# A planned kernel whose planner is told of the eight transfers in flight, and may give early small work to GpSimd

## The chip, the cores and the metric

The kernel runs on one core of a Trainium2 chip. The metric is device time in microseconds (us) of one execution, as a median over runs. The engines are named as in the profile: PE is TensorE, DVE is VectorE, ACT is ScalarE, POOL is GpSimd, SP is SyncE, which here only issues transfers (DMAs). All matrix products are in float32, and most of them are made of three products of high and low parts.

## The reference

```python
scores = (q @ k^T) / 8                          # 4 batches x 8 heads, 576 x 576, head size 64
keep   = scores >= max(scores) - tau            # per row
attn   = softmax of the kept scores             # exp(s - max) / (sum + 1e-9)
x = concat over heads of (attn @ v)             # 2304 tokens x 512
h = x @ w_in;   x = (h * clip(h + 3, 0, 6) / 6) @ w_out          # 512 -> 2048 -> 512
h = x @ w_in2;  x = (h * sigmoid(1.702 * h)) @ w_out2            # 512 -> 2048 -> 512
```

## The kernel before

**Stages.** Attention is worked in 16 units of two heads (function `unit`). The first four (`u < FULL`) are the early ones: their scores are plain float32 products of `g` (or `kqv`) with the keys `kqv` (L653, L669), and their probabilities are turned by TensorE (L743) and multiplied with the values (L785). The other twelve split q and k into high and low parts (L637) and partly turn the probabilities through DRAM (L754, L757, L759; their products are L802). Beside attention the first half of the first feed-forward layer is computed (`moe_a`, L862 and L887), then its second half (`moe_b`), then the second layer (`moe2`, L1024 and L887). The weights come as 64-bit words and are decoded to floats by `decode`: a load `wrawstg` (L470), two ACT copies (L480, and L427 in place), three DVE steps (a clamp L481, a shift L483, a merge L484) and a POOL addition.

**One score tile.** The function `soft` follows a score product into one of two PSUM tiles `ps`: the row maximum (R, DVE, L685), the threshold `th` = maximum - tau (TH, L686, 128x1), the exponential (X, ACT, L688) and the masking with its sum (M, DVE, L689), which needs `th` and frees the `ps` tile. So PE can be at most two score tiles ahead of M.

**What sets the order.** Nothing is scheduled by hand. `Plan` holds every operation with an engine, a planned cost and what it reads and writes. `order` runs the plan as a list schedule, `latest` turns it round into priorities, and `settle` repeats both under a list of numbers (KICKS and SHAKES): a positive number disturbs the priorities as a random seed, a negative one, -n, moves operation n to the engine that its `alt` names. The result is one fixed order for each engine, and engines wait for each other by semaphores only. The dictionary `PORT` names the operations of DVE and POOL that the plan keeps from overlapping.

**Fillers.** After planning, `fill` puts small products of the constant `two` (L1187) wherever the planned order leaves PE without work, about one for every 0.216 us of the planned gap less 0.3 us. They compute nothing that is used. Before has 35 of them, 70 records in the trace, since a float32 product of this kind has two.

**Transfers.** `move` adds an issue on SP (or ACT) and the transfer itself. The built program gives every transfer one of eight semaphores in turn, and an issue waits until the transfer that had the same semaphore, eight issues earlier, has landed. In `order` of before a transfer waits for its issue and its data alone. SP takes its list in order, so one late transfer can hold all that stand behind it.

## Time and profile before

| what | us |
|---|---|
| median of 3 runs | 1064.68 (1060.67 to 1068.29) |
| profiled execution, its own time | 1060.78 |
| span of the profiled execution | 1059.0 |
| PE busy | 1045.0 |
| fillers among that (L1187, 70 records) | 11.2 |
| DVE / ACT / POOL busy | 718.5 / 631.0 / 518.9 |

A busy PE is the union of its matmul records, and their ends are modelled; a wait of PE shows as a gap, or as an idle time with its releaser behind a row. In the 40 slices of the page PE stands at 8 in the first and at 9 in all that follow but the last, which ends after the last product. The granted TensorE clock is 9 (0.98 to 1.00) throughout.

### The profile page before, as it was taken

How to read it: one execution, taken by the hardware profiler on the slowest of the kernel's cores; microseconds unless marked ns; L12 is line 12 of the kernel's file. 1: busy time of each engine (PE TensorE's matmuls, PEld its weight loads, DVE VectorE, ACT ScalarE, POOL GpSimd, SP SyncE). 2: the span in 40 equal slices, each digit the busy share in tenths (PEclk: the TensorE clock that was granted, in tenths of full speed). 3: DMA queues.
4: the chain of work that ended last, by engine and by line, in shares of the span. 5: the costliest groups of instructions: out<-in, count | busy, mean ns of one | idle time of the engine just before them, and what ended most of it. 6: DMA issues, size and time to landing. Idle time of an engine off the chain costs nothing.

```text
span 1059.0 us, 20374 instructions
## 1 busy us (share of the span) xinstructions
PE 1045.0 (99%) x7470; PEld 955.4 (90%) x7470; DVE 718.5 (68%) x1542; ACT 631.0 (60%) x1272; POOL 518.9 (49%) x597
## 2 busy tenths in 40 slices
PE   8899999999999999999999999999999999999998
PEld 6677888899879988999999999989988989899888
DVE  7898888767777872677765333888787585563544
ACT  4889677666666664666554224766665675344433
POOL 4579888776867663755574225441422431001000
PEclk9999999999999999999999999999999999999999
DMA  7434465645564535445744211527553561320202
GB/s 229 117 101 149 136 182 164 191 139 156 160 183 127 157 110 173 131 144 178 218 145 139 60 59 59 165 80 228 166 169 119 178 193 35 119 86 35 95 1 76
DMA packets 87109, 141.79 MB, mean 134 GB/s; under 512 B 8544, under 2 KB 51168, under 8 KB 85472
## 3 DMA queue, kind: packets, MB, share of 16 engines
q1 hardware_dynamic: 86784, 140.41, 44.2%
q8 instruction: 59, 0.97, 0.4%
q14 instruction: 42, 0.34, 0.1%
q10 hardware_dynamic: 224, 0.07, 0.0%
HBM read 97.32 MB, written 43.12 MB: 133 GB/s over the span
## 4 chain that ended last, share of the span: by engine, by line
PE 88%; DVE 4%; DMA 3%; ACT 2%; issue 1%; SPq 1%; POOL 1%; ACTq 0%; DVEq 0%; POOLq 0%
PE py L887 26%; PE pm L862 19%; PE pm L1024 15%; PE pm L887 9%; PE ps L637 6%; PE pm L802 6%; PE pm L743 5%; PE pm L785 1%; PE ps L669 1%; DMA kqv<-in_k_dram 1%; DMA wrawstg<-in_w1i_dram 1%; DVE outlring L430 1%; DVE e L689 0%; DMA wrawstg<-in_w1o_dram 0%; SPq L589 0%
## 5 line engine op out<-in xcount | busy, mean ns | idle before, releaser
L887 PE MATMUL py<-g,outhring 128*128 128x512 f32 (+2 forms) x1152 | 286.4, 336 | 0.7 <-DVE g L430 0.7
L887 PEld LDWEIGHTS py<-g,outhring 128*128 128x128 f32 x1152 | 192.4, 188 | 16.6 <-DVE g L430 1.9
L887 PE MATMUL py<-g,outlring 128*128 128x512 f32 (+2 forms) x576 | 193.2, 335 | 0.0
L862 PE MATMUL pm<-xh,inhring 128*128 128x256 f32 (+1 forms) x512 | 153.4, 300 | 0.2
L862 PE MATMUL pm<-xl,inhring 128*128 128x256 f32 (+1 forms) x512 | 150.8, 295 | 0.0
L862 PE MATMUL pm<-xh,inlring 128*128 128x256 f32 (+1 forms) x512 | 150.7, 294 | 0.0
L1024 PE MATMUL pm<-outhring,inhring 128*128 128x256 f32 x512 | 144.7, 283 | 0.5 <-ACT p L427 0.4
L1024 PE MATMUL pm<-outlring,inhring 128*128 128x256 f32 x512 | 143.9, 281 | 0.1
L1024 PE MATMUL pm<-outhring,inlring 128*128 128x256 f32 x512 | 143.6, 280 | 0.0
L685 DVE TENSOR_REDUCE nm<-ps 128x1 f32<-128x576 f32 x144 | 107.0, 752 | 35.8 <-PE ps L637 30.1
L430 POOL TENSOR_TENSOR g<-t,g 128x256 fp32r<-128x256 f32 (+1 forms) x104 | 87.8, 850 | 81.7 <-ACT g L427 74.8
L887 PEld LDWEIGHTS py<-g,outlring 128*128 128x128 f32 x576 | 108.1, 188 | 10.1
L689 DVE SCALAR_TENSOR_TENSOR e<-ps,th,e 128x576 f32<-128x576 f32 x128 | 102.4, 810 | 21.5 <-ACT e L688 20.1
L874 DVE SCALAR_TENSOR_TENSOR t<-t,pm 128x256 f32<-128x256 f32 (+1 forms) x128 | 57.2, 450 | 86.7 <-ACT t L873 86.2
L430 POOL TENSOR_TENSOR g<-tc,g 128x512 fp32r<-128x512 f32 x24 | 32.5, 1355 | 161.9 <-ACT g L427 160.0
L688 ACT ACTIVATE e<-ps,nm 128x576 f32<-128x576 f32 x128 | 92.7, 739 | 31.9 <-DVE nm L685 27.8
L430 POOL TENSOR_TENSOR wmstg<-wmstg,wrstg 128x512 uint32<-128x512 uint32 x48 | 66.9, 1393 | 91.1 <-DVE wmstg L484 69.5
L873 ACT ACTIVATE t<-pm,half 128x256 f32<-128x256 f32 (+1 forms) x128 | 63.4, 500 | 80.3 <-PE pm L862 77.6
L887 PE MATMUL pm<-g,outhring 128*128 128x256 f32 (+1 forms) x512 | 107.3, 300 | 0.0
L1024 PEld LDWEIGHTS pm<-outhring,inhring 128*128 128x128 f32 x512 | 96.7, 189 | 5.1 <-ACT p L427 1.0
L1024 PEld LDWEIGHTS pm<-outlring,inhring 128*128 128x128 f32 x512 | 96.8, 189 | 3.2 <-DVE outlring L430 0.3
L862 PEld LDWEIGHTS pm<-xh,inhring 128*128 128x128 f32 x512 | 96.5, 188 | 2.1 <-PE pm L1187 0.7
(114 smaller groups left out, 2397.2 us busy)
## 6 DMA issues: line engine op xcount, KB each, us to landing
turned<-tr SPq DMA_DIRECT2D x12, 1024.0 KB, 3.9
et<-turned SPq DMA_DIRECT2D x48, 256.0 KB, 6.2
wrawstg<-in_w1i_dram SPq DMA_DIRECT2D x16, 512.0 KB, 4.0
wrawstg<-in_w1o_dram SPq DMA_DIRECT2D x16, 512.0 KB, 3.6
wrawstg<-in_w2i_dram SPq DMA_DIRECT2D x16, 512.0 KB, 3.8
wrawstg<-in_w2o_dram SPq DMA_DIRECT2D x16, 512.0 KB, 3.9
qk<-in_k_dram SPq DMA_DIRECT2D x24, 288.0 KB, 3.8
qk<-in_q_dram SPq DMA_DIRECT2D x24, 288.0 KB, 3.4
```

The source lines that it names most:

```text
L430: return lambda: (nc.vector if eng == DVE else nc.gpsimd).tensor_tensor(out=o(), in0=a(), in1=b(), op=op)
L637: nc.tensor.matmul(ps.t[:, i, :SH], qss[hd].t[:, q0:q0 + P], w[hd].t[:, i * SH:(i + 1) * SH], start=a, stop=z)
L685: add(DVE, 672, K("R", s), "R", lambda: nc.vector.tensor_reduce(out=nm.t[:, c], in_=ps.t[:, :, :SH], op=ALU.max, axis=AX.XY, negate=True), ...
L688: add(ACT, 624, K("X", s), "X", lambda: nc.scalar.activation(out=ev(), in_=ps.t[:, :, :SH], func=ACTF.Exp, bias=nm.t[:, c]), [ps, (nm, s)] ...
L689: add(DVE, 736, K("M", s), "M", lambda: nc.vector.scalar_tensor_tensor(out=ev(), in0=ps.t[:, :, :SH], scalar=th.t[:, c], in1=ev(), op0=ALU ...
L743: nc.tensor.transpose(pt.t[:kn, o:o + P], e_of[s].t[:, keys(k)], id_b.t)
L802: nc.tensor.matmul(pv[p].t[64 * hd:64 * hd + 64, :CH[p][1]], v_(k, hd), x, start=k == 0, stop=k == 4)
L862: nc.tensor.matmul(ph.t[:, :n], a, v, start=(cc == 0 and i == 0), stop=(cc == KC - 1 and i == 2))
L873: add(ACT, 93 + act(n), K("RL"), "RL", lambda: nc.scalar.activation(out=tt_(), in_=pt(), func=ACTF.Relu, scale=1.0 / 6.0, bias=half_b.t), ...
L874: add(DVE, dve(n), K("GT"), "GT", lambda: nc.vector.scalar_tensor_tensor(out=tt_(), in0=tt_(), scalar=1.0, in1=pt(), op0=ALU.min, op1=ALU. ...
L887: nc.tensor.matmul(py.t[:, :n], a, v, start=(st and i == 0), stop=(sp and i == 2))
L1024: nc.tensor.matmul(o.t[:, :n], u.t[:, ws], v.t[:, xv], start=(st and kk == 0 and i == 0), stop=(sp and kk == 1 and i == 2), skip_group_che ...
```

## The change

1. `order` gets a list of SP's transfers. An issue on SP waits in the plan for the transfer eight issues earlier (LANES = 8) and the latency of a transfer. Transfers of ACT's queue are not in that list.
2. At the start the first unit's keys go through ACT's queue; tau and the first half of q, which were there, go through SP's.
3. The planned size factor of a weight load is 1.7 where it was 1.4.
4. TH gets POOL as its other engine (it was ACT).
5. KICKS and SHAKES are other numbers, so every engine's order is another. Thirteen of their moves put work on POOL: 8 thresholds TH, 3 scalings of q (128x256, 128x512, 128x384) and 2 clamps (128x512). There are 49 fillers where there were 35. Otherwise the engines have the same instructions.

```diff
-CAPS, BANKS = (2, 2, 3, 4), 4
+CAPS, BANKS, LANES = (2, 2, 3, 4), 4, 8
...
 KICKS = (
-    838826498, 483723856, 648238324, 249340718, 651019405, 283728814,
+    185786211, 131810043, 105014005, 620353508, 1009081972, 162601711, 396413032, 546200070, 621028586, -184, 226485323, 975211561,
...
+        issued, late, fin = [], [], [None] * n
...
+            if e == SP and cost[o] and len(issued) >= LANES:
+                x = fin[issued[-LANES] + 1]
+                if x is None:
+                    late.append(o)
+                    continue
+                if x + LAT[DMA, SP] > t:
+                    est[o] = x + LAT[DMA, SP]
+                    heappush(p, (est[o], o))
+                    continue
...
+            if e == SP and cost[o]:
+                issued.append(o)
+            elif e == DMA:
+                fin[o] = end
+                for h in late:
+                    heappush(pend[SP], (est[h], h))
+                late = []
...
-    move(-30000, "tau", 4 * P, lambda: nc.scalar.dma_start(out=tau_b.t, in_=tau), [], [tau_b], ACT)
+    move(-30000, "tau", 4 * P, lambda: nc.sync.dma_start(out=tau_b.t, in_=tau), [], [tau_b])
...
-        move(time - 15000, "WL", 8 * P * DM * 1.4, load, [], [raw])
+        move(time - 15000, "WL", 8 * P * DM * 1.7, load, [], [raw])
...
-                eng, q = (ACT, nc.scalar) if u + hd == 0 else (SP, nc.sync)
...
+            eng, q = (ACT, nc.scalar) if u == 0 else (SP, nc.sync)
+            move(K("ld") - 8000 * (u == 0), "ldk", 512 * S * 1.4, lambda rows=rows, q=q: q.dma_start(out=f32(khb.t)[:, :S], in_=k2.rearrange("b h p s -> (b h p) s")[rows:rows + P]), [], [khb], eng)
...
-                (ACT, 200, lambda: nc.scalar.activation(out=th.t[:, c], in_=nm.t[:, c], func=ACTF.Identity, scale=-1.0, bias=nt_b.t)))
+                (POOL, 189, lambda: nc.gpsimd.tensor_scalar(out=th.t[:, c], in0=nm.t[:, c], scalar1=-1.0, scalar2=nt_b.t, op0=ALU.mult, op1=ALU.add)))
```

The order of the changed kernel is shown at three places. Its lines stand 10 or 11 further down in the file (L470 is now L481, L480 is L491, L1187 is L1198).

SP's list around the third weight load (`wrawstg_333` before, `wrawstg_336` now; `kqv` holds q and the values, `qk` raw q or k). Before:

```order
L623 DMA kqv_182<-in_vp_dram 128x640
L596 DMA kqv_173<-in_q2_dram 64x256
L596 DMA kqv_173<-in_q2_dram 64x64
L596 DMA kqv_178<-in_q2_dram 64x320
L596 DMA kqv_178<-in_q2_dram 64x64
L596 DMA kqv_178<-in_q2_dram 64x256
L623 DMA kqv_317<-in_vp_dram 128x640
L605 DMA qk_327<-in_k2_dram 128x576
L470 DMA wrawstg_333<-in_w1i_dram 128x4x256
```

and now:

```order
L607 DMA kqv_172<-in_q2_dram 64x64
L634 DMA kqv_181<-in_vp_dram 128x640
L607 DMA kqv_172<-in_q2_dram 64x256
L607 DMA kqv_172<-in_q2_dram 64x320
L634 DMA kqv_325<-in_vp_dram 128x640
L481 DMA wrawstg_336<-in_w1i_dram 128x4x256
L607 DMA kqv_177<-in_q2_dram 64x64
L607 DMA kqv_177<-in_q2_dram 64x320
L607 DMA kqv_177<-in_q2_dram 64x256
L617 DMA qk_360<-in_q2_dram 128x576
L616 DMA qk_359<-in_k2_dram 128x576
```

The weight load is moved ahead of one unit's three pieces of q and of one raw k, 448 KB together.

ACT's list around the same load's first copy, its exponential and the copy that empties a PSUM bank (`et<-pm`). Before:

```order
L427 ACTIVATE xr0_392<-pm_361 128x256
L480 ACTIVATE wmstg_396<-wrawstg_333 128x512
L427 ACTIVATE wrawstg_333<-wrawstg_333 128x512
L688 ACTIVATE e_415<-ps_389,nm_402 128x576
L746 ACTIVATE et_165<-pm_410 128x512
```

and now:

```order
L438 ACTIVATE xr0_388<-pm_362 128x256
L491 ACTIVATE wmstg_390<-wrawstg_336 128x512
L438 ACTIVATE wrawstg_336<-wrawstg_336 128x512
L438 ACTIVATE inhring1_408<-wmstg_309 128x512
L699 ACTIVATE e_417<-ps_384,nm_401 128x576
L757 ACTIVATE et_166<-pm_393 128x512
```

The weight copies still stand ahead of the exponential and of the emptying, and one more copy (`inhring1_408`) has come between.

PE's list near the end of the eighth unit, which in the trace of before is the stretch from 195 to 208 us (`pm<-two` are fillers, `ps<-kqv` scores, `pm<-id,e` turns). Before:

```order
L887 MATMUL pm<-g,outlring_1594 128x320
L743 MATMUL pm<-id,e 128x128 x16
L637 MATMUL ps<-kqv 128x288 x4
L743 MATMUL pm<-id,e 64x128 x4
L887 MATMUL pm<-g,outhring_1578 128x320 x2
L887 MATMUL pm<-g,outlring_1594 128x320
L802 MATMUL pm<-et,kqv 64x256 x10
L802 MATMUL pm<-et,kqv 64x320 x10
L637 MATMUL ps<-kqv 128x288 x12
L1187 MATMUL pm<-two 128x128 x2
```

and now:

```order
L898 MATMUL pm<-g,outlring_1608 128x320
L1198 MATMUL pm<-two 128x128 x4
L648 MATMUL ps<-kqv 128x288 x8
L754 MATMUL pm<-id,er 128x128 x4
L754 MATMUL pm<-id,er 64x128
L1198 MATMUL pm<-two 128x128 x5
L648 MATMUL ps<-kqv 128x288 x4
L754 MATMUL pm<-id,e 128x128 x16
L754 MATMUL pm<-id,e 64x128 x4
L1198 MATMUL pm<-two 128x128 x3
L813 MATMUL pm<-et,kqv 64x256 x10
```

The feed-forward products (L887) that stood between the scores before have been used up earlier, and twelve fillers stand there. Five more fillers come much later, ahead of a product into `py` that in the trace of before runs at 684 us; the four fillers of before at 119 to 129 us and two at 315 us are gone, and at the start there are 19 where there were 16.

## Rows read from the trace of the kernel before

**Rows 1.** The page, parts 1 and 4: busy time by engine; chain that ended last.
```profile
PE 1045.0 (99%) x7470; PEld 955.4 (90%) x7470; DVE 718.5 (68%) x1542; ACT 631.0 (60%) x1272; POOL 518.9 (49%) x597
...
PE 88%; DVE 4%; DMA 3%; ACT 2%; issue 1%; SPq 1%; POOL 1%; ACTq 0%; DVEq 0%; POOLq 0%
```
**Rows 2.** Windows of 26 us: length, busy us (count) by engine, clock, DMA share, GB/s.
```profile
0.00:26.00 26.00, 21.66 (x117) 16.80 (x118) 20.66 (x57) 13.16 (x21) 12.10 (x31) 1.00 0.78 228
26.00:52.00 26.00, 23.35 (x156) 16.91 (x156) 22.58 (x56) 22.16 (x43) 14.26 (x18) 1.00 0.40 112
52.00:78.00 26.00, 25.70 (x192) 20.73 (x190) 24.08 (x61) 23.53 (x48) 20.67 (x26) 1.00 0.35 104
78.00:104.00 26.00, 25.32 (x193) 19.41 (x190) 22.50 (x54) 24.71 (x50) 24.22 (x26) 1.00 0.49 144
104.00:130.00 26.00, 24.84 (x195) 22.32 (x194) 23.89 (x61) 17.45 (x33) 22.12 (x31) 1.00 0.43 138
...
182.00:208.00 26.00, 26.00 (x200) 21.05 (x199) 19.09 (x45) 15.85 (x31) 20.19 (x27) 1.00 0.65 188
```
**Rows 3.** Timeline of PE, 0 to 42 us: start, length, line, idle before and releaser.
```profile
1.38 3.78 PE L1187 MATMUL pm<-two 128*128 128x128 f32 x16 [1.38 <-DVE two L449]
...
9.34 2.27 PE L653 MATMUL ps<-kqv,g 128*128 128x288 f32 x8 [1.00 <-DVE th L686]
...
13.35 1.21 PE L653 MATMUL ps<-kqv,g 128*128 128x288 f32 x4 [0.85 <-PE pm L1187]
...
18.41 1.24 PE L653 MATMUL ps<-kqv,g 128*128 128x288 f32 x4 [0.70 <-DVE e L689]
19.98 1.24 PE L653 MATMUL ps<-kqv,g 128*128 128x288 f32 x4 [0.33 <-DVE e L689]
...
29.13 0.68 PE L731 MATMUL pm<-id,bt 128*128 128x128 f32 x4 [1.72 <-POOL bt L723]
...
37.08 1.21 PE L653 MATMUL ps<-kqv,g 128*128 128x288 f32 x4 [0.21 <-PE pm L743]
...
40.22 1.24 PE L653 MATMUL ps<-kqv,g 128*128 128x288 f32 x4 [0.61 <-DVE e L689]
```
**Rows 4.** Timeline of POOL, 0 to 30 us: the second half of the first `bt`.
```profile
22.86 0.30 POOL L723 TENSOR_SCALAR bt<-rc 128x128 f32<-128x128 f32 x1
```
**Rows 5.** Chain of waits, 0 to 62 us: start, us, what.
```profile
8.22 8.02 DMA kqv<-in_k_dram
...
20.51 6.06 DMA wrawstg<-in_w1i_dram
```
**Rows 6.** Timeline of ACT, 18 to 32 us.
```profile
26.66 0.68 ACT L480 ACTIVATE wmstg<-wrawstg 128x512 f32<-128x512 f32 x1 [2.70 <-DMA wrawstg<-in_w1i_dram]
...
28.41 1.07 ACT L746 ACTIVATE et<-pm 128x512 f32<-128x512 f32 x2
```
**Rows 7.** Groups by form: line, shapes, count, busy us, mean ns, idle before.
```profile
L686 DVE TENSOR_SCALAR th<-nm,nt 128x1 f32<-128x1 f32 x144 | 28.6, 207 | 1.3
...
L610 POOL TENSOR_SCALAR qk<-qk,sc 128x576 f32<-128x576 f32 x24 | 18.0, 749 | 8.9 <-DMA qk<-in_q_dram 8.4
...
L695 POOL TENSOR_SCALAR sm<-sm 128x4 f32<-128x4 f32 x4 | 1.1, 284 | 8.1 <-DVE e L689 7.9
```
**Rows 8.** Timeline of all engines, 24 to 62 us: two clamps, and POOL beside one.
```profile
29.40 0.42 DVE L481 TENSOR_SCALAR wmstg<-wmstg 128x512 f32<-128x512 f32 x1
...
34.35 1.28 POOL L430 TENSOR_TENSOR inlring<-wmstg,inhring 128x512 fp32r<-128x512 f32 x1
34.38 1.53 DVE L481 TENSOR_SCALAR wmstg<-wmstg 128x512 f32<-128x512 f32 x1
```
**Rows 9.** Timeline of PE, 54 to 60 and 125 to 130 us: fillers, and a product behind.
```profile
55.65 2.72 PE L1187 MATMUL pm<-two 128*128 128x128 f32 x22
...
125.64 0.61 PE L1187 MATMUL pm<-two 128*128 128x128 f32 x4
127.04 0.74 PE L743 MATMUL pm<-id,er 128*64 128x128 f32 x5 [0.79 <-POOL er L702]
```
**Rows 10.** Groups of the whole span: POOL's addition in a weight's decoding.
```profile
L430 POOL TENSOR_TENSOR wmstg<-wmstg,wrawstg 128x512 uint32<-128x512 uint32 x16 | 21.6, 1353 | 13.1 <-DVE wmstg L484 8.9 <-ACT et L746 2.6 <-ACT wmstg L480 1.3
```

More of the change, by code (lines that the diff above doesn't have):

```diff
@@ L587, in unit @@
                 add(POOL, 100, K("ld"), "qz", lambda o=o, c=256 + 64 * hd: nc.gpsimd.memset(f32(qhb.t)[o, c:c + 64], 0.0), [], [(qhb, ("z", hd))])
-                eng, q = (ACT, nc.scalar) if u + hd == 0 else (SP, nc.sync)
-                move(K("ld") - 6000 * (u == 0), "ldq", 256 * 256 * 1.5, lambda r=r, c=256 * hd, h=2 * j + hd, q=q: q.dma_start(out=f32(qzb.t)[r, c:c + 256], in_=q2[b, h, :64, :256]), [], [(qzb, (hd, 0))], eng)
+                move(K("ld") - 6000 * (u == 0), "ldq", 256 * 256 * 1.5, lambda r=r, c=256 * hd, h=2 * j + hd: nc.sync.dma_start(out=f32(qzb.t)[r, c:c + 256], in_=q2[b, h, :64, :256]), [], [(qzb, (hd, 0))])
             rows = (b * H + 2 * j) * P + 64
-            move(K("ld") - 8000 * (u == 0), "ldk", 512 * S * 1.4, lambda rows=rows: nc.sync.dma_start(out=f32(khb.t)[:, :S], in_=k2.rearrange("b h p s -> (b h p) s")[rows:rows + P]), [], [khb])
+            eng, q = (ACT, nc.scalar) if u == 0 else (SP, nc.sync)
+            move(K("ld") - 8000 * (u == 0), "ldk", 512 * S * 1.4, lambda rows=rows, q=q: q.dma_start(out=f32(khb.t)[:, :S], in_=k2.rearrange("b h p s -> (b h p) s")[rows:rows + P]), [], [khb], eng)
             for c, n, regions in ((0, 256, [("z", 0), (0, 0)]), (256, 256, [("z", 1), (1, 0)])) if u == 0 else ((0, 512, [("z", 0), (0, 0), ("z", 1), (1, 0)]),):
```

38 rows, old and new, of the table SHAKES are left out of this document.

## The prediction

> **What bounds the kernel now.** I read the page first, its busy shares and its chain [rows 1]. PE is busy for 1045.0 us of 1059.0, and the chain of waits lies on PE for 88%. The products of both kernels are the same, so the change can only take away PE's idle time and its fillers, or add to them. Then I cut the span into windows of 26 us to see where PE is idle [rows 2]. From 182 to 208 us PE is busy for 26.00 of 26 us, and most windows of the later span look like that one. The first five windows show 21.66, 23.35, 25.70, 25.32 and 24.84, so 9.13 us are idle in the first 130 us, 1.38 of them before the first product [rows 3]. That leaves 7.75 us to win there, beside fillers, of which 3.78 us run while the first inputs are on their way [rows 3].
>
> Third, PE's timeline shows which waits make up the first two windows [rows 3]: 1.00, 0.85, 0.70 and 0.33 us before 20 us, then 1.72 us before L731 at 29.13, then 0.21 and 0.61. Three of the seven name a DVE step of the softmax, and the 0.85 falls behind fillers ahead of the same kind of score product, so I count it with them. The large one names POOL's `bt`, but the second half of that tile was written at 22.86 [rows 4]. So the releaser is another one, and the chain of waits tells which [rows 5]: a key load of 8.02 us holds SP's list until 16.24, and the third weight load is issued at 20.51 and lands 6.06 us later. ACT's timeline goes on from there [rows 6]: its first copy of that weight waits 2.70 us for the load, and only after it, at 28.41, comes the copy that empties the PSUM bank PE needs. **So until 29 us the pace is set by transfers, through ACT; DVE's and PE's waits before that are slack in that chain.**
>
> **The change part by part.** The sum is made against the profiled execution, 1060.78 us (span 1059.0).
>
> *The weight load.* 448 KB of transfers that stood ahead of it now stand behind it. The first window moves 228 GB/s with its DMA engines busy for 0.78 [rows 2], so 458,752 bytes are 2.0 us, and the load should land at about 24.6 instead of 26.6. ACT now makes one more copy before the exponential, 0.6 us by its neighbours of the same shape (0.68 at 26.66 [rows 6]). PE's wait of 1.72 [rows 3] shrinks by 2.0 - 0.6 = 1.4 us. Bounds: 0, if the eight places hold SP and not the bytes; 1.7, the whole wait.
>
> *Work taken off DVE.* Eight thresholds at 207 ns [rows 7] are 1.66 us; three scalings and two clamps at about 0.42 each [rows 8] are 2.1. So 3.8 us leave DVE, nearly all in the first 55 us, where it is busy for 43 of 52 [rows 2]. Before 29 us this wins nothing, because the chain goes by the transfers. After it PE's waits are 0.21 and 0.61 [rows 3]. One of the clamps that move is the one that took 1.53 us at 34.38 [rows 8], ahead of both. I take half, 0.4 us. Bounds: 0, and 3.7 if the four early waits go too (2.88 + 0.82).
>
> *The same work on POOL.* A threshold is nearest to the 128x4 addition, 284 ns; the five wider steps are at most 749 each [rows 7]. That is at most 2.3 + 3.7 = 6.0 us on an engine that is idle for 13.9, 11.7 and 5.3 us in the first three windows [rows 2]. Cost 0, covered by that idle time. Where the cover is gone is the second rival.
>
> *Start.* Tau and q now go through SP, the first keys through ACT. The second half of the first q is issued two places later, about 0.6 us each, and there are 9 fillers ahead of the first score instead of 8 (3.78 us / 8 = 0.47 each [rows 3]). The first scores may be 0.5 us late, but the chain to 29 us starts at SP's transfers and not at the scores. Cost 0; bound 0.5.
>
> *Fillers.* Eleven took 2.72 us at 55.65 [rows 9], so one costs 0.25. The three added at the start lie in PE's waits there, cost 0. Of the rest, 17 are added (12 near 200 us, 5 near 684) and 6 taken away. Where PE would wait anyway a filler costs nothing: behind those at 125.64 PE waited 0.79 us more [rows 9]. Where it would not, the price is full: near 200 us PE of before was busy throughout [rows 2]. So the added ones cost 0 to 4.2, the missing ones give 0 to 1.5. I take half of 4.2, since each of the two cases has its row, and all of 1.5: +0.6. If the holes that the plan saw are real, they outlast their fillers; with 0.5 us for each of four groups (the 0.79 is the nearest row) that is 2.0 more, and the upper bound is 6.2.
>
> *The larger planned size of weight loads, and the eight places known to the plan,* change nothing on the chip but the order, which is what was costed.
>
> **Sum:** -1.4 - 0.4 + 0 + 0 + 0.6 = -1.2 us. The profiled execution is 3.9 us below the median shown, 1064.68, and the lowest run, 1060.67, is there too; the mean of the three runs and the profiled one is 1063.6. From that the forecast is 1063.6 - 1.2 = **1062 us**, its own range 1058 to 1066 by the spread of the runs shown.
>
> **Rivals.**
>
> *The early idle time goes as a whole.* If the plan's new knowledge fits every transfer, all 7.75 us of idle time in the first 130 us go, at +0.6 for fillers: 1063.6 - 7.15 = 1056. For it: the chain to 29 us hangs on transfers. Against it: from 52 to 130 us DVE, ACT and POOL are each busy for 17 to 25 of 26 us [rows 2], and no transfer order mends that. Chance 0.15.
>
> *Thresholds wait in POOL's list.* POOL takes its list in order, and three thresholds of the second unit now stand close to a weight addition of 1353 ns [rows 10]. A threshold behind one comes 1.35 + 0.28 - 0.21 = 1.4 us later, M with it, and the score tile too. It decides where the addition starts before the row maximum ends, and PE has already used its two tiles, as in the rows that name `e` [rows 3]. Five of eight: 7.0 us; with the weight load's gain used up and the fillers' +0.6: 1063.6 + 7.6 = 1071. All eight: 1075 to 1076. Against it: POOL is the less busy of the two there [rows 2]. Chance 0.12.
>
> *The change does not do what it says.* The eight places hold SP in the first 30 us only, and the plan now makes room for waits that the chip does not have. No gain, fillers at full price less six: +2.7, with the holes +4.7: 1066 to 1068. For it: near 200 us nothing waited. Chance 0.13.
>
> *POOL holds DVE.* The clamp that started at 34.38, 0.03 us after a POOL step of 1.28, took 1.53 instead of 0.42, and ended 0.28 after it [rows 8]. If each step that moves to POOL holds a DVE step so, up to 6.0 us come back on DVE; half of that on PE, less the weight load's gain and with the fillers: 1063.6 + 3.0 - 1.4 + 0.6 = 1066. Against it: the eight thresholds are short. Chance 0.05. The Trainium skill has this as a rule ("SBUF — State Buffer", the section on its two separate sides): VectorE in its two-port modes and GpSimd take a shared port pair as a lock for a whole instruction, and the later one fully blocks. By that rule each meeting of the two would look like the 1.53 us, and the time would be this rival's; the trace agrees on the one meeting shown.
>
> **How the numbers follow.** The forecast has 0.55, the rivals 0.15, 0.12, 0.13 and 0.05. About 1% (10.6 us) is what a measurement of this kernel can tell from no change. Below 1054.0 lies only the lower half of the first rival's spread: 0.08. Above 1075.3 lies the far end of the second: 0.04. The rest, 0.88, is no change. The range is 1054 to 1071; it leaves out about 0.07 below and 0.08 above, which are the far ends of those two rivals, and the runs alone spread over 7.6 us.
>
> **What would show it.** In the changed kernel's trace: the third weight load's first ACT copy (L491) starting near 24.6 with its wait under 1 us; PE's wait before the first L742 under 0.6; the windows from 0 to 52 us with 2 to 3 us less idle time or fillers; thresholds on POOL (L698) ending before DVE's mask asks for them; and, against the fourth case, PE idle behind the twelve fillers near 200 us. It is wrong if PE's idle time in the first 130 us grows above 9.1 us, if DVE's mask names POOL as its releaser for more than 2 us in all, or if PE shows waits of several us after 130 us, where before had none.

## The result, and the profile after

The change makes the kernel slower by a little. The median is 1070.82 us (seven runs, 1069.79 to 1074.24) against 1062.78 for seven runs of before beside them: ratio 1.0074, interval 1.0061 to 1.0087, or +7.9 us (6.5 to 9.3). That is inside the 1% called "no change", but clearly above zero, and 8.8 us above the forecast, which had expected a small gain. The profiled execution took 1069.95 us, span 1068.2.

The page after, busy time and chain, against [rows 1]:

```profile
PE 1050.3 (98%) x7498; PEld 959.2 (90%) x7498; DVE 720.7 (67%) x1529; ACT 630.9 (59%) x1272; POOL 520.5 (49%) x610
...
PE 85%; DVE 6%; DMA 2%; ACT 2%; POOL 2%; issue 2%; SPq 0%; DVEq 0%; POOLq 0%; ACTq 0%
```

The span grew by 9.2 us: for 5.3 of them PE is busier (3.1 of that are fillers, which went from 11.2 to 14.3), and for 3.9 it is idle. The windows after, with the columns of [rows 2]:

```profile
0.00:26.00 26.00, 21.30 (x120) 16.75 (x121) 18.38 (x48) 13.90 (x23) 12.93 (x37) 1.00 0.75 225
26.00:52.00 26.00, 24.36 (x170) 18.34 (x170) 22.84 (x54) 22.91 (x44) 20.13 (x26) 1.00 0.42 125
52.00:78.00 26.00, 25.28 (x178) 19.51 (x175) 22.81 (x55) 21.74 (x44) 20.78 (x24) 1.00 0.29 89
78.00:104.00 26.00, 26.00 (x198) 19.88 (x196) 23.16 (x54) 24.67 (x50) 22.85 (x27) 1.00 0.47 143
104.00:130.00 26.00, 25.03 (x192) 22.59 (x191) 23.71 (x58) 18.06 (x33) 23.67 (x31) 1.00 0.43 141
...
182.00:208.00 26.00, 25.05 (x190) 20.65 (x190) 19.15 (x48) 16.84 (x34) 17.19 (x25) 1.00 0.60 184
676.00:702.00 26.00, 24.99 (x165) 22.52 (x164) 20.68 (x38) 16.38 (x32) 9.32 (x8) 1.00 0.32 91
```

In the first 130 us PE is idle for 8.03 us instead of 9.13, less of a gain than forecast: in the first 52 us idle time fell by 0.65, not by 2 to 3. Behind 130 us it rose from 4.87 to 9.87. Some of that stands in the window from 182, where before had none, and some near 676, where before stood at

```profile
676.00:702.00 26.00, 25.81 (x172) 23.62 (x172) 21.67 (x38) 18.09 (x37) 13.84 (x11) 1.00 0.44 128
```

A window also hides what the engine was busy with. A better measure is a progress curve: count PE's products other than fillers by their columns (plain float32 ones twice), and ask at equal work how late PE is against the profiled execution of before. Lag in us, from the traces, columns by the time before reaches that work (the kernels under the first are explained below):

| kernel | 34 | 159 | 183 | 203 | 457 | 733 | 980 |
|---|---|---|---|---|---|---|---|
| the change | -1.6 | -0.6 | -0.8 | +4.1 | +2.5 | +7.8 | +9.0 |
| e1_late | +1.7 | +1.2 | +1.1 | +1.6 | +1.7 | +6.6 | +5.7 |
| e2_early | +0.3 | +1.5 | +1.3 | +6.9 | +8.4 | +8.3 | +11.4 |
| e3_eighth | +0.5 | +0.8 | +1.9 | +6.2 | +6.8 | +7.0 | +10.2 |
| e4_first | -1.6 | +1.7 | +1.9 | +1.9 | +2.3 | +2.2 | +4.9 |
| b1_front | +0.4 | +0.6 | +1.7 | +4.8 | +5.3 | +5.7 | +6.8 |
| b2_back | -0.4 | -0.2 | -0.3 | +3.7 | +5.2 | +5.2 | +7.2 |
| p2_moe2 | +0.2 | +1.7 | +1.7 | +1.7 | +1.7 | +6.0 | +8.6 |
| c3_ends | -2.1 | -1.5 | -1.5 | -1.5 | -1.6 | -1.7 | -2.4 |

Two steps stand out in the change: +4.9 between 183 and 203 us, and +5.3 between 457 and 733 (nearly all from 666 to 711).

**The start.** PE's timeline after, 0 to 42 us, against [rows 3]:

```profile
1.38 3.66 PE L1198 MATMUL pm<-two 128*128 128x128 f32 x18 [1.38 <-DVE two L460]
6.47 2.21 PE L664 MATMUL ps<-kqv,g 128*128 128x288 f32 x8 [1.44 <-POOL g L605]
...
27.84 0.61 PE L742 MATMUL pm<-id,bt 128*128 128x128 f32 x4
...
39.14 1.24 PE L664 MATMUL ps<-kqv,g 128*128 128x288 f32 x4 [1.56 <-DVE e L700]
```

The wait of 1.72 us before the first `bt` product is gone, and ACT's first copy of that weight, against [rows 6], starts without waiting:

```profile
24.45 0.68 ACT L491 ACTIVATE wmstg<-wrawstg 128x512 f32<-128x512 f32 x1
```

But the first scores come at 6.47 instead of 5.25, for a reason that POOL's timeline shows: its first scaling of q is queued behind its memsets.

```profile
5.21 0.63 POOL L577 MEMSET et<- 64x640 f32 x1
5.94 0.48 POOL L605 TENSOR_SCALAR g<-g,sc 128x256 f32<-128x256 f32 x1
```

And the 1.56 at 39.14 goes back to a clamp in POOL's list, which a threshold stands behind. POOL and DVE, 31 to 35 us:

```profile
31.61 1.93 POOL L493 TENSOR_SCALAR wmstg<-wmstg 128x512 f32<-128x512 f32 x1
...
31.90 0.82 DVE L700 SCALAR_TENSOR_TENSOR e<-ps,th,e 128x576 f32<-128x576 f32 x1
...
33.64 0.26 POOL L698 TENSOR_SCALAR th<-nm,nt 128x1 f32<-128x1 f32 x1
...
33.94 0.82 DVE L700 SCALAR_TENSOR_TENSOR e<-ps,th,e 128x576 f32<-128x576 f32 x1 [1.22 <-POOL th L698]
```

This is the only time that a mask waits for a threshold on POOL: 1.2 us in the whole span.

**From 194 to 206 us**, PE after. In before this stretch has no idle time [rows 2] and no filler (the first stands at 208.14):

```profile
194.64 0.77 PE L648 MATMUL ps<-kqv 128*128 128x288 f32 x4 [0.29 <-DVE e L700]
...
197.09 1.05 PE L1198 MATMUL pm<-two 128*128 128x128 f32 x8
198.29 1.51 PE L648 MATMUL ps<-kqv 128*128 128x288 f32 x8 [0.15 <-DVE e L700]
...
200.19 1.28 PE L1198 MATMUL pm<-two 128*128 128x128 f32 x10
201.86 0.76 PE L648 MATMUL ps<-kqv 128*128 128x288 f32 x4 [0.39 <-DVE e L700]
...
204.64 0.83 PE L1198 MATMUL pm<-two 128*128 128x128 f32 x6
```

and before, the third score tile behind the multiplication of the seventh unit's values (which ends at 187.40) and the start of the eighth unit's:

```profile
191.12 0.68 PE L637 MATMUL ps<-kqv 128*128 128x288 f32 x4
...
201.43 5.07 PE L802 MATMUL pm<-et,kqv 128*64 128x256 f32 x40
```

The fillers stand where feed-forward products of L898 (before: L887) stood. The number of products in the traces explains that. Those of the first layer's two lines (L873 and L898, before: L862 and L887) do not need the softmax of the unit that is being worked, and 384 of them are made before the eighth unit's values are multiplied. Between the seventh and the eighth multiplication before has 48 left and takes 14.0 us; the change has 24 left and takes 15.4. It had made 360 by then, before 336, and was already 18 ahead near 137 us (231 against 213). PE's work done early shows as a lead in the table, and the lead is lost where the stretch lasts as long as the softmax chain whatever PE has to do: 24 products of 0.146 us are 3.5 us, and the stretch itself is 1.3 us longer, together the +4.9.

The chain of waits after begins there with a transfer, and POOL, DVE and PE follow it:

```profile
177.93 7.41 DMA qk<-in_q_dram
```

**From 666 us**, in the second layer, SP issues the read-back of `xa` at 694.52, where before issued it at 684.15, and DVE waits for it, and PE for ACT behind it. SP before, then SP, DVE and PE after:

```profile
684.15 0.37 SPq L960 DMA_DIRECT2D xa<-x2d  x1
```

```profile
694.52 0.37 SPq L971 DMA_DIRECT2D xa<-x2d  x1
...
698.94 0.69 DVE L441 TENSOR_TENSOR xt<-xa 128x512 f32<-128x512 f32 x1 [3.56 <-DMA xa<-x2d]
...
708.44 0.39 PE L1035 MATMUL pm<-outhring,inhring 128*128 128x256 f32 x1 [1.39 <-ACT u L438]
```

### The profile page after: what moved, and what is told of

Same layout as the page of the kernel before. It is cut to its first block, busy times and chain, and to the rows that moved or that the text cites. A ratio compares the mean times of both kernels' runs of the same rounds, so it can differ in the third digit from the quotient of the medians.

```text
span 1068.2 us, 20427 instructions
## 1 busy us (share of the span) xinstructions
PE 1050.3 (98%) x7498; PEld 959.2 (90%) x7498; DVE 720.7 (67%) x1529; ACT 630.9 (59%) x1272; POOL 520.5 (49%) x610
## 4 chain that ended last, share of the span: by engine, by line
PE 85%; DVE 6%; DMA 2%; ACT 2%; POOL 2%; issue 2%; SPq 0%; DVEq 0%; POOLq 0%; ACTq 0%
PE py L898 25%; PE pm L873 18%; PE pm L1035 13%; PE pm L898 9%; PE ps L648 6%; PE pm L813 5%; PE pm L754 5%; PE pm L796 2%; PE ps L680 1%; DVE outlring L441 1%; DMA xa<-x2d 1%; DVE e L700 1%; PE ps L664 1%; DMA qk<-in_q_dram 1%; DVE nm L696 1%
## 5 line engine op out<-in xcount | busy, mean ns | idle before, releaser
L898 PE MATMUL py<-g,outhring 128*128 128x512 f32 (+2 forms) x1152 | 287.2, 336 | 0.5 <-DVE g L441 0.4
L898 PEld LDWEIGHTS py<-g,outhring 128*128 128x128 f32 x1152 | 192.3, 188 | 16.3 <-DVE g L441 1.5
L898 PE MATMUL py<-g,outlring 128*128 128x512 f32 (+2 forms) x576 | 193.3, 336 | 0.0
L873 PE MATMUL pm<-xh,inhring 128*128 128x256 f32 (+1 forms) x512 | 153.4, 300 | 0.1
L873 PE MATMUL pm<-xl,inhring 128*128 128x256 f32 (+1 forms) x512 | 150.8, 295 | 0.0
L873 PE MATMUL pm<-xh,inlring 128*128 128x256 f32 (+1 forms) x512 | 150.7, 294 | 0.0
L898 PEld LDWEIGHTS py<-g,outlring 128*128 128x128 f32 x576 | 108.1, 188 | 10.2
L898 PE MATMUL pm<-g,outhring 128*128 128x256 f32 (+1 forms) x512 | 107.4, 301 | 0.0
L1035 PEld LDWEIGHTS pm<-outhring,inlring 128*128 128x128 f32 x512 | 97.5, 190 | 0.0
```

The lines of the kernel that those rows point to most:

```text
L873: nc.tensor.matmul(ph.t[:, :n], a, v, start=(cc == 0 and i == 0), stop=(cc == KC - 1 and i == 2))
L898: nc.tensor.matmul(py.t[:, :n], a, v, start=(st and i == 0), stop=(sp and i == 2))
L1035: nc.tensor.matmul(o.t[:, :n], u.t[:, ws], v.t[:, xv], start=(st and kk == 0 and i == 0), stop=(sp and kk == 1 and i == 2), skip_group_che ...
```

## The experiments

Most kernels mix the two plans. `PIECES` gives, in order, whose plan is followed (True is before's) and until which planned time in ns; every operation takes the engine, the bank (where it is free) and the fillers of the plan it is taken from, and stands a little later where its inputs are not made yet. `HOME` puts operations that the change gave to POOL back on DVE in their place, `FILLERS` says which fillers stay, `MOVES` puts one operation right behind another (last number 1) or right ahead of it (0). Times are given as the ratio to before, which ran beside each of them, with the interval, and in us of 1063. The lines below show the settings of several kernels under each other; the words behind # only say whose they are. Parts 1, 3 and 5 of the change (the eight places, the planned size of a load, the numbers) act through the order alone, and no run separates them.

### Which stretch costs: four mixtures

```diff
+PIECES = ((True, 656000), (False, 1e12))                   # e1_late
+PIECES = ((False, 410000), (True, 1e12))                   # e2_early
+PIECES = ((True, 162000), (False, 204000), (True, 1e12))   # e3_eighth
+PIECES = ((False, 138000), (True, 1e12))                   # e4_first
```

> The order of before for everything it starts until the last stretch of the first layer's second half (about 664 us), then the order of the change for the whole second layer; the queues of the start as in before, none of the thirteen moved operations on POOL, 5 of the 14 additional fillers of the later span. Theory (the new order of the second layer waits in real holes, at 676 to 711 and near 788 us): the two traces' curves of PE's work against time differ by 3.0 us at 664 and 9.2 at the end, so 6.1 us slower than before, 1068.9 where before is 1062.8. Rival A (the thirteen operations on POOL and the late start cost it): none of them is here, so no change, 1062.8. Rival B (fillers at full price): five at 0.25, 1.3 us, 1064.1.

> The order of the change until the end of attention (about 416 us), with its queues at the start, all thirteen operations on POOL and its fillers there, then the order of before. Theory: the curves stand 2.5 us apart at 424 us, so 2.5 us slower than before, 1065.3. Rival A (operations on POOL and start): the whole 8 to 9 us, 1071. Rival B (fillers at full price, 12 near 200 us less the six taken away): 1.5 us plus 0.5 for the start, 1064.8; it is told apart from the theory by the trace alone: PE's waits between 190 and 205 us and the 2 us given back at 290 to 340.

> The order of before, but of the change for what its plan starts between 162 and 204 us (some 170 to 212 us on the chip: the softmax of the eighth unit and the first expert products around it), then before again. Twelve more fillers, none of the thirteen moved operations, start as in before. Theory: 4.9 us slower than before, 1067.7, with POOL's wait for a load of q near 185 us and PE's waits for the mask (L700's counterpart) between 193 and 202. Rival A: no change, 1062.8. Rival B (fillers alone): 12 at 0.22 are 2.6, 1065.4, with no waits beside them.

> The order of the change until 138 us of its plan (about 145 us), with its queues, all thirteen operations on POOL, its nine fillers ahead of the first score; then the order of before to the end. Theory (the change's stated parts are worth about what was forecast, the loss is all behind them): the curves stand at -0.7 us there, so 1062.1. Rival A (POOL and start cost the 8 us): 1070 or more. Rival B (fillers): 1063.

Measured: e1_late 1066.11 us, 1.0022 (1.0012 to 1.0033), +2.3; e2_early 1069.76, 1.0058 (1.0041 to 1.0075), +6.2; e3_eighth 1072.00, 1.0079 (1.0062 to 1.0097), +8.4; e4_first 1064.97, 1.0013 (1.0002 to 1.0025), +1.4. No theory of the four came out: 2.3 for 6.1, 6.2 for 2.5, 8.4 for 4.9, and a loss of 1.4 for a gain of 0.7.

The halves add up: 2.3 + 6.2 = 8.5 against 7.9. But the weights are not those of the two single traces. The early part costs more than they said and the second layer less; the 42 us around the eighth unit cost 8.4 by themselves. The table shows why: from 733 us on, e2_early, e3_eighth and e4_first follow before's order and still lose 2.7 to 3.2 us up to 980 us against the profiled execution of before. So that execution (1060.78 of a median of 1062.78) was most likely a lucky one in its last third, and the change's trace was compared with it.

e4_first shows the loss of a lead too. It has the change's 18 products in advance at 137 us and then before's lists; from the sixth multiplication to the seventh 45 products are left to it where before has 63, the stretch takes 17.6 us against 17.9, PE is idle for 1.8 us of it, and the curve goes from -0.7 at 145 us to +1.7 at 159.

### The eighth unit, split

```diff
+PIECES = ((True, 162000), (False, 182000), (True, 1e12))   # b1_front
+PIECES = ((True, 182000), (False, 204000), (True, 1e12))   # b2_back
```

> The order of before, but of the change for what its plan starts between 162 and 182 us (some 169 to 189 us on the chip), then before again: the front half of the stretch that cost 8 us. Theory (the loss is made here: the second layer products L898 of the expert, PE's reserve, are issued ahead of the softmax steps that they would have covered, and exponential, normalisation and transposition of the eighth unit come later on ACT, POOL and DVE; the waits that show behind 190 us are its bill): most of the 8 us, 4 to 6 slower than before, 1068 to 1070. Rival (the back half, with its twelve fillers, holds the cause): 0 to 1, 1064 to 1065.

> The order of before, but of the change for what its plan starts between 182 and 204 us, then before again: the back half, with the fillers that the change puts there. Theory: before has its reserve and its softmax in time here, so the fillers are the whole cost, up to 12 at 0.22, 2.6 us, less where they fall into waits: 0 to 2.6 slower, 1064 to 1066.6. Rival (the cause is here): 4 to 6 slower, 1068 to 1070.

Measured: b1_front 1068.61, 1.0050 (1.0035 to 1.0065), +5.3; b2_back 1068.93, 1.0055 (1.0039 to 1.0072), +5.8. b1_front takes before's order from 182 us, with no filler in the stretch, and yet PE waits, since the change's front has used 24 products of it. PE of b1_front, 192 to 206 us:

```profile
195.99 1.45 PE L694 MATMUL ps<-kqv 128*128 128x288 f32 x8 [1.24 <-DVE e L746]
...
200.43 0.66 PE L800 MATMUL pm<-id,er 128*128 128x128 f32 x4 [0.24 <-POOL er L759]
...
203.03 1.89 PE L800 MATMUL pm<-id,e 128*128 128x128 f32 x15 [0.74 <-POOL e L759]
```

b1_front came out as expected. Its stretch takes 13.7 us with 24 products, before's 14.0 with 48: 3.5 us less work there saves 0.4.

b2_back came out as its rival said (4 to 6 us). It keeps all 48 products, takes the change's order of the later lists, and its stretch lasts 18.0 us instead of 14.0. PE of b2_back, the two places that are shown of before above (its seventh multiplication ends at 187.14):

```profile
194.38 0.68 PE L694 MATMUL ps<-kqv 128*128 128x288 f32 x4
...
205.18 5.07 PE L859 MATMUL pm<-et,kqv 128*64 128x256 f32 x40
```

The third score tile starts 7.2 us behind the seventh multiplication, after 39 of the 48 products; in before 3.7 us, after 15. From there to the eighth multiplication it is 10.8 us against 10.3. The same 10.7 to 10.9 us stand in the traces of the change, m2_nofill, f1_lists and g2_reserve, with 24 products or 48 and with fillers or without, so from the third score tile on the softmax chain sets the pace. Of b2_back's 4.0 us some 3.5 come from PE's own list, which puts 24 more products ahead of that tile, and 0.5 from a longer chain. In the change, with 24 products left, 15 stand ahead of it as in before. So the two halves are not two separate costs of the change: each shows 24 products in a place where nothing needs them, once a unit too early and once ahead of the scores. That fits their not adding (8.4, not 11.1).

### Fillers, lists, and the work on POOL

```diff
+    return t < 100000                                      # FILLERS, m2_nofill: 19 go
+    return True                                            # HOME, m1_home: all 13 on DVE
+    return o.n == 184                                      # HOME, g1_first: first scaling
+MOVES = ((1582, 1272, 1), (1253, 1203, 0), (1262, 1199, 0))  # f1_lists
```

> The order of the change without its 19 filler products behind 100 us of its plan (14 near 200 us, 5 near 684); the 30 of the first 62 us stay. Theory (the holes are there whatever fills them): the same as the change to 0.7 us, 8 us slower than before, 1072. Rival B (fillers at full price): 19 at 0.22 to 0.25 are 4.2 to 4.8 us faster than the change, 1067 to 1068.

> The order of the change, place for place, but the thirteen operations that it moved to POOL (eight thresholds, three scalings of q, two clamps) are done by DVE again. Theory (the order costs the time; of the moved work only the first scaling counts, since it stands behind memsets in POOL's list and made the first scores 1.2 us late): 1 us faster than the change, 7 us slower than before, 1071. Rival A (POOL costs it): all 8 us come back, 1064. Rival D (the moved work pays, DVE being busy for 43 of the first 52 us): 1 to 3 us slower than the change, 1073 to 1075.

> The changed kernel with one operation moved back: the first q scaling of 128x256 that the change gave to POOL is done by DVE, at its place in the order. Theory (it stands behind memsets in POOL's list, so the first scores start at 6.4 instead of 5.3 us, and PE, idle for over a microsecond by then, runs them at half speed in some executions): first scores at 5.3, 1.2 to 2.5 us faster than the change, 5.5 to 6.7 us slower than before, 1069 where before is 1063. Rival (the start has slack until the third weight load): no change against the changed kernel, 1071.

> The order of the change, with three operations moved in two lists near 176 to 187 us: on POOL the q scaling that waits for a load (L621's counterpart) stands behind the two normalisations instead of ahead of them (and two more behind those), and on ACT two exponentials each one place earlier, ahead of a copy to et. PE's, DVE's and SP's lists are unchanged. Theory (the eighth unit is slow because its normalisation stands behind a load in POOL's list): DVE's wait for it, 2.2 us in the trace of the change, goes and PE's later waits shrink, 2 to 3 us faster than the change, so 5 to 6 us slower than before, 1069. Rival C (PE's own order is the cause: its expert products stand too early there, and nothing covers the softmax later): no change against the changed kernel, 8 us slower than before, 1072.

In f1_lists POOL does its scaling of q behind its normalisations, and ACT two exponentials one place earlier.

Measured: m2_nofill 1068.28, 1.0049 (1.0029 to 1.0069), +5.2; m1_home 1068.94, 1.0059 (1.0038 to 1.0081), +6.3; g1_first 1070.46, 1.0065 (1.0052 to 1.0078), +6.9; f1_lists 1070.50, 1.0059 (1.0036 to 1.0082), +6.3. Each interval overlaps that of the change, so none of the four is shown to be a cause, and gains of 1 to 2.7 us are not excluded. For m2_nofill the times do not decide: it is 2.7 us below the change (some 0 to 5), between its theory (0.7) and the full price of the fillers (4.2 to 4.8). Its trace decides for the two places. PE from 196 to 206 us:

```profile
196.42 0.76 PE L694 MATMUL ps<-kqv 128*128 128x288 f32 x4 [0.29 <-DVE e L746]
...
200.06 1.50 PE L694 MATMUL ps<-kqv 128*128 128x288 f32 x8 [1.05 <-DVE e L746]
...
203.62 0.76 PE L694 MATMUL ps<-kqv 128*128 128x288 f32 x4 [1.51 <-DVE e L746]
```

The holes are real and stay without their fillers: the stretch takes 15.6 us, with them 15.4, and near 684 us the curve rises by 2.3 us, with them 2.2. In f1_lists POOL's wait for the load is gone and the third score tile starts 3.7 us behind the seventh multiplication, as in before and not 4.5 as in the change; its stretch takes 14.5 us. The gain of 1.6 us that the times show has an interval that includes none.

### Giving the products back

```diff
+MOVES = ((817, 1299, 1), (818, 817, 1), (819, 818, 1), (820, 828, 1),
+         (821, 1309, 1), (822, 821, 1), (823, 1335, 1), (824, 823, 1))  # g2_reserve
+    return not 189000 < t < 198000                         # FILLERS: 12 go
```

> The changed kernel with 24 expert products (eight groups of three, L898, of one accumulation) moved on PE from the interval ahead of the attention-value products of the seventh unit to the places that before gives them, among the scores and transpositions behind it; their copy and store follow them; the 12 fillers there are left out. Theory (the interval lasts as long as the eighth unit's softmax, 14 to 15 us, whatever PE has to do in it; 24 products fewer in it are 24 x 0.146 = 3.5 us lost, and the fillers and waits only fill that room): 3.5 to 4.5 us faster than the change, 4 us slower than before, 1067. Rival (exponential and normalisation late in ACT's and POOL's lists are the cause): no more than 1 us faster, 1070, with PE waiting between the products.

> The changed kernel with all three places undone: every moved operation on DVE, the 24 products moved as in the kernel before this one, and from 656 us of the plans on (the second layer) the order of before. Theory (the three places are the whole difference): -1.6, -4 and -2.3 of the 8 us, so as fast as before to 1 us, 1062 to 1064. Rival (something else of the change's order between 44 and 410 us costs too): 2 us or more slower than before, 1065 or above.

g3_both adds all operations on DVE and `PIECES = ((False, 656000), (True, 1e12))`.

Measured: g2_reserve 1070.87, 1.0072 (1.0060 to 1.0084), +7.7; g3_both 1065.57, 1.0033 (1.0022 to 1.0044), +3.5. Both theories failed, and g3_both met its rival (2 us or more slower than before). Moving 24 products behind the seventh multiplication opens another hole before it. PE of g2_reserve, 160 to 190 us:

```profile
178.38 0.77 PE L694 MATMUL ps<-kqv 128*128 128x288 f32 x4 [0.35 <-DVE th L743]
182.96 0.79 PE L694 MATMUL ps<-kqv 128*128 128x288 f32 x4 [1.32 <-DVE e L746]
184.07 1.33 PE L694 MATMUL ps<-kqv 128*128 128x288 f32 x8 [0.33 <-DVE e L746]
```

The seventh unit's stretch does not get shorter (17.7 us with 39 products, 17.8 with 63), so its softmax chain sets its pace too. And the products did not come back to the places of before: 27 of the 48 stand ahead of the third score tile, where before has 15, it starts 5.6 us behind the seventh multiplication, and the eighth unit's stretch takes 16.5 us. 18 of the products had been spent earlier still, before 141 us. A repair would have to start there and restore the places too; that was not tried.

### The start alone, and before with both good ends

```diff
+PIECES, OLD_START = ((True, 1e12),), False                 # s1_queues: only the queues
+PIECES = ((False, 44000), (True, 1e12))                    # c2_start, ops on DVE
+PIECES = ((False, 44000), (True, 207000), (False, 327000), (True, 1e12))  # c1_pieces
+PIECES = ((False, 44000), (True, 820000), (False, 1e12))   # c3_ends
```

> The order of before, place for place, with the queues of the start alone changed: tau and the first half of the first q through SP, the first keys through ACT. Theory as forecast (the third weight load is issued two places nearer, and PE's wait of 1.72 at 29 us shrinks): 1.0 to 1.4 us faster than before, 1062.6. Rival E (the first scores come later by as much as the load comes earlier, and the start sets the pace): no change, 1064, with the first score product later than 5.25 us.

> The order of the change for what its plan starts in the first 44 us, with its queues, but with every moved operation on DVE, then the order of before. Theory (the early transfers and order are worth what was forecast, and only the first scaling on POOL loses it): the curve of the kernel with all operations on DVE stands 2.6 us ahead of before at 47 us, so 2 to 2.6 us faster than before, 1061.5. Rival (before's later order has slack for none of it, so the early gain is used up by the next wait, as it was where the queues alone were changed): no change, 1064.

> The best pieces by the curves: the start as in the kernel before this one, the order of before from 44 to 207 us of the plans, of the change from 207 to 327 (it has neither the two fillers nor the wait of before near 310 us), and of before from there. Theory: 2.6 and 1.5 us ahead, 3 to 4 us faster than before, 1060.5. Rival: no change, 1064; or, if the seams cost what one of them seemed to cost near 146 us (up to 1.9 each), 1064 to 1067.

> The start of the change with every moved operation on DVE (first 44 us), the order of before from there to 820 us of the plans, then the change's order to the end. Theory: 1.6 us faster by the start as timed before; the curves of five traces with the change's order fall by 1.2 to 1.7 us between 854 and 866 us against a rise of 0 to 2.4 with the order of before, so 1 to 2 us more, 2.6 to 3.6 us faster than before, 1060. Rival (the last stretch's gain is a debt that the same order made earlier in the second layer): as fast as the start alone, 1061.4.

Measured: s1_queues 1064.13, 0.9996 (0.9980 to 1.0011), -0.4; c2_start 1061.39, 0.9985 (0.9972 to 0.9998), -1.6; c1_pieces 1063.57, 1.0006 (0.9994 to 1.0017), +0.6; c3_ends 1060.46, 0.9973 (0.9962 to 0.9985), -2.9 (1.6 to 4.0). The first 44 us of the change with the small work on DVE are a gain, as expected; the queues alone are not (their lead of 1.1 us at 34 is 0.3 at 138). The stretch from 207 to 327 us, where the change's own curve falls 1.4 us, gives nothing as a piece: c1_pieces is 2.2 us behind c2_start. What the end adds in c3_ends, 1.3 us to c2_start, is within the intervals. **c3_ends beats both kernels.** Its first windows, where before had 21.66 and 23.35:

```profile
0.00:26.00 26.00, 22.22 (x123) 17.48 (x124) 20.11 (x57) 14.52 (x24) 10.71 (x31) 1.00 0.81 230
26.00:52.00 26.00, 25.10 (x170) 17.93 (x168) 23.88 (x60) 22.86 (x44) 16.91 (x21) 1.00 0.42 126
```

### The second layer

```diff
+MOVES = ((4783, 4677, 1),)                                 # p1_xa: last read of xa earlier
+PIECES = ((True, 656000), (False, 716000), (True, 1e12))   # p2_moe2
```

> The changed kernel with one DVE operation moved: the last subtraction that reads the first xa of the second layer (outlring<-xa, at 692.66 us in the trace of the change) stands where the order of before has it, about 5 us earlier, so that SP can issue the next load of xa at about 688 instead of 694.5. Theory (DVE stands 3.56 us in its list waiting for that load, and PE's waits at 706 to 711 us, 2.6 to 4 us in all, are the bill): the load lands by 693, DVE's wait goes, 2 to 2.5 us faster than the change, 5.5 us slower than before, 1068.5 where before is 1063. Rival (the expert work ahead of it sets the pace, and the load has slack): no change against the changed kernel, 1071.

> The order of before, but of the change for what its plan starts between 656 and 716 us (the first 45 us of the second layer on the chip), then before again. Theory (the loss of the second layer is made here, 4.0 to 5.5 us in all five traces that have this order, and what follows gives some back): 4 to 5 us slower than before, 1067 to 1068, more than the 2.3 us of the kernel that keeps the change's order to the end. Rival (a later stretch takes up the delay, since before waits there too): 2.3 us or less, 1065.

Measured: p1_xa 1069.20, 1.0065 (1.0051 to 1.0079), +6.9; p2_moe2 1068.15, 1.0054 (1.0040 to 1.0068), +5.7. p2_moe2 shows that the first 60 us of this layer cost by themselves; with the rest of the change's order behind them (e1_late) they cost 2.3, so that rest gives back about 3 (the intervals are 4.3 to 7.2 and 1.3 to 3.5). p1_xa shows one part of the mechanism. SP and DVE of p1_xa:

```profile
690.56 0.37 SPq L1017 DMA_DIRECT2D xa<-x2d  x1
...
696.37 0.68 DVE L487 TENSOR_TENSOR xt<-xa 128x512 f32<-128x512 f32 x1
```

DVE's wait of 3.56 us and PE's 1.39 at 708 are gone, and the curve's rise from 457 to 733 is 3.8 instead of 5.3. The time, 1.0 us less where 2 to 2.5 were expected, is within the intervals, and what makes the other 3.8 stays open.

## Why the prediction was wrong, step by step

**The weight load: right.** The copy was forecast near 24.6 and stands at 24.45; PE's wait before the first `bt` product is gone. What that is worth by itself was not timed.

**Work taken off DVE, "0.4 us": not shown.** m1_home, which puts all of it back on DVE, is not slower than the change but 1.6 us faster, within the intervals.

**The same work on POOL, "cost 0, covered by that idle time": mis-sized.** The clamp was bounded by 749 ns and takes 1932, in all 16 records of the eight traces that have it on POOL:

```profile
L493 POOL TENSOR_SCALAR wmstg<-wmstg 128x512 f32<-128x512 f32 x2 | 3.9, 1932 | 0.2
...
L698 POOL TENSOR_SCALAR th<-nm,nt 128x1 f32<-128x1 f32 x8 | 2.6, 329 | 3.8 <-DVE nm L696 3.6
```

The nearest row by shape was of another operation: both take two constants, but the scaling multiplies twice and the clamp takes a maximum and a minimum.

**The start, "bound 0.5": mis-sized.** The prediction counted places in SP's list and not POOL's own, where memsets stand ahead. The first scores are 1.2 us late, and in three of the traces they end 2.9 to 3.3 us late, as below. g1_first, which starts them at 5.39, gains 1.0 us, within the intervals. All that is planned before 138 us is +1.4 timed (e4_first), against the -1.8 that the first two steps promised; the 18 products made too early are part of it.

**Fillers: the step that failed.** "Near 200 us PE of before was busy throughout" was read as: added fillers cost their full price, or nothing. The trace could not show the third case, that the plan had taken away the work which kept PE busy. The prediction's third rival named holes that outlast their fillers, but at 0.5 us for each of four, with the products of PE taken as the same in every stretch. They are the same in sum and not in place: 24 products had moved out, 3.5 us, and the stretch grew by 1.3 us besides, 0.75 of them in the wait ahead of the third score tile, which is gone in f1_lists, and 0.6 in the chain behind it. Without the fillers the holes stay (m2_nofill). The term was +0.6, with a bound of 6.2; the stretch costs 4.9 us of the lag in the trace and, with all between 138 and 410 us, 4.8 timed. That no repair brought the time back (g2_reserve) leaves a part of this account argued.

**"After 130 us", the second layer: not predicted.** The only term there was five fillers. Timed it is +2.3 (e1_late), and the trace of m2_nofill loses as much there without them.

**The sum:** +1.4 before 138 us (e4_first), +4.8 from there to 410 (e2_early less e4_first), +2.3 in the second layer: 8.5, against 7.9 measured; the first and the last term have intervals of 2.2 to 2.4 us, the middle one, a difference, of some 4.4. Which list order adds the 0.6 us to the eighth unit's chain stays open. That 1070.82 lies inside the stated range, by 0.2 us, is luck: the upper end was set for thresholds that wait on POOL.

**The rivals.** Thresholds waiting in POOL's list happened once of eight, for 1.2 us on DVE and 1.56 on PE. POOL holding DVE was seen at one of the moved steps, a scaling of q. POOL and DVE of the change, then DVE and POOL of g1_first:

```profile
25.97 0.58 POOL L609 TENSOR_SCALAR kqv<-kqv,sc 128x384 f32<-128x384 f32 x1
...
26.08 0.74 DVE L492 TENSOR_SCALAR wmstg<-wmstg 128x512 f32<-128x512 f32 x1
```

```profile
25.91 0.40 DVE L538 TENSOR_SCALAR wmstg<-wmstg 128x512 f32<-128x512 f32 x1
...
25.97 0.79 POOL L655 TENSOR_SCALAR kqv<-kqv,sc 128x384 f32<-128x384 f32 x1 [0.29 <-DMA kqv<-in_q_dram]
```

Where POOL's scaling starts first (the change and five more traces) DVE's clamp takes 0.73 to 0.74 us instead of 0.42, and where the clamp starts first (g1_first and f1_lists) the scaling takes 0.79 to 0.81 instead of 0.58. That is 0.2 to 0.3 us, not the 6.0 of the rival. A mask beside POOL's clamp took its usual 0.82 us at 31.90; with PSUM among its inputs it may not be one of the steps which the Trainium skill ("SBUF — State Buffer", on the two sides) has blocked. The pair of scaling and clamp agrees with that rule, by which the one that starts first blocks the other. The early idle time did not go as a whole. Of the signs named for it, the copy, the wait before the first `bt` product and seven of the eight thresholds came as named, the 2 to 3 us less in the first 52 us did not. Of the three signs named as proof of error, only the last came true: waits of PE behind 130 us, where its idle time rose from 4.87 us, which the prediction had called none, to 9.87.

## What to carry to other kernels

A stretch without idle time can owe that to finite work that another order will spend elsewhere: before costing a new plan, count by stretch how many of the independent products it leaves beside each dependent chain, and how many of them it puts ahead of the chain's first link. When a step moves to another engine, read what stands ahead of it in that engine's list, and take its price from the same operation, not from the same shape. A single profiled execution can be off by 3 us in one third of the span, so timed mixtures of the two orders, and not the difference of two traces, tell where the time went.

## What was not expected of the hardware

The first score products run at half their pace in some executions. PE from 0 to 12 us in m2_nofill:

```profile
1.38 4.21 PE L1242 MATMUL pm<-two 128*128 128x128 f32 x18 [1.38 <-DVE two L506]
6.58 3.77 PE L710 MATMUL ps<-kqv,g 128*128 128x288 f32 x8 [0.98 <-POOL g L651]
```

The same eight products take 2.21 us in the change, 3.98 in f1_lists, 4.21 in e2_early, with starts 0.48 us apart instead of 0.24; the spacing is that of the lower level, 1.2 GHz. In f1_lists, e2_early and m2_nofill PE had been idle for about 1 us just before. In e4_first it had too (1.03 us) and the products ran at full pace, and in b1_front it had not and they took 3.23. The profile's column of the granted clock reads 1.00 for that window, but that is no reading: in each of the 20 traces the first record of the clock begins where the spacing narrows, or in a wait just ahead of it, at 4.31 us in the change, 5.23 in before, 9.78 in m2_nofill, 10.10 in f1_lists and 10.92 in e2_early. The starts of the first fillers, 0.21 us apart in all 20 and 0.11 behind that, say the same: PE begins at the lower level, and that before has 1.00 throughout holds from 5.23 us on. The Trainium skill ("TensorE: Matmul & The Clock Gate", Part 1) says that the array starts at half rate and that the moment of the rise varies between runs, which these traces agree with.

A clamp (maximum, minimum) of 128x512 floats takes 1.93 us on POOL and 0.42 on DVE [rows 8], a ratio of 4.6, while a scaling (two multiplications) of 128x576 takes 0.75 on POOL. The wait of POOL for the eighth unit's q load was 2.50 us in the change, 2.87 in m2_nofill, 3.19 in e2_early and none in f1_lists, where the scaling stands later in the list.
